# A chunked linear-attention kernel followed by a squared-relu feed-forward: eight heads at once, attention and feed-forward in one pipeline, x kept in SBUF

## The chip, the cores and the metric

The kernel runs on one core of a Trainium2 chip. The metric is device time in microseconds (us). Profiles are taken by the hardware profiler on the same core; a profile's span is about 2 us shorter than the device time.

Engines, as the profile names them: PE is TensorE's matmuls, PEld its weight loads, DVE is VectorE, ACT is ScalarE, POOL is GpSimd, SP is SyncE, which only issues DMA here. SBUF is the on-chip memory that tiles live in, PSUM the one that this program's matmuls write to, HBM the large memory that loads come from. A *slot* is one pass of the changed kernel's main loop.

## The reference

Four batches, eight heads, 768 tokens, head dimension 48. Attention keeps one 48x48 state per batch and head; its output is reshaped to x (3072 tokens by 384) and goes through two matrices.

```python
for t in range(S):                                       # attention, r k v: (4, 8, 768, 48)
    cur = einsum('bhd,bhe->bhde', u * k[t], v[t])        # the bonus term
    y[t] = einsum('bhd,bhde->bhe', r[t], state + cur)
    state = w * state + einsum('bhd,bhe->bhde', k[t], v[t])
x = y.transpose(0, 2, 1, 3).reshape(3072, 384)
h = x @ w_in                                             # 384 x 2048
g = maximum(h, 0) ** 2
out = g @ w_out                                          # 2048 x 384
```

Both kernels compute attention in chunks of 128 tokens: scores inside a chunk by matmul and mask, earlier chunks by the state, the decay folded into r and k beforehand. A *unit* below is 128 tokens of one batch. There are 24 units, of eight heads each.

## The kernel before

One head at a time: 192 bodies like this one, with 48 columns in most operations.

```python
for c in range(NCH):
    for b in range(B):
        for h in range(H):
            nc.sync.dma_start(out=rt, in_=r[b, h, t0 : t0 + C, :])      # kt, vt alike
            nc.vector.tensor_tensor(Rw, rt, wp_pos[h], ALU.mult)        # 128 x 48
            nc.vector.tensor_tensor(Kd, kt, wp_neg[h], ALU.mult)
            nc.vector.tensor_tensor(rku, rt, kt, ALU.mult)
            # ... bonus sum du, transposes of Rw and Kd, copy to SBUF ...
            nc.tensor.matmul(out=AT_p, lhsT=KdT, rhs=RwT, start=True, stop=True)
            nc.vector.tensor_tensor(AT, AT_p, smask, ALU.mult)          # 128 x 128
            # ... diagonal, two output matmuls, state update ...
            nc.sync.dma_start(out=xT[...], in_=yT)                      # x goes to HBM
actx.close()
nc.gpsimd.dma_start(out=w_in_sb, in_=moe_w_in...)                       # weights only now
nc.gpsimd.dma_start(out=w_out_sb, in_=moe_w_out...)
for t in range(NG):                                                     # 6 groups of 512 tokens
    nc.sync.dma_start(out=xt, in_=xT[...])
    for f in range(NF):                                                 # 16
        # three matmuls 128x128x512 into hps
        nc.scalar.activation(gr, hps, AF.Relu)
        nc.vector.tensor_tensor(g, gr, gr, ALU.mult)
        # four matmuls 128x128x384 into ops
```

Of the kernel before, what the change touches and what calls it, by code (L numbers as in the profile page):

```python
# [8 lines left out]
F32 = mybir.dt.float32  # L9
BF16 = mybir.dt.bfloat16  # L10
# [5 lines left out]
def kernel(  # L16
# [11 lines left out]
    nc = tc.nc  # L28
# [3 lines left out]
    dm = H * D  # L32
    dff = moe_w_in.shape[1]
    ntok = B * S

    xT = nc.dram_tensor("xT_scratch", (dm, ntok), BF16, kind="Internal").ap()

    const = ctx.enter_context(tc.tile_pool(name="const", bufs=1))
    ident = const.tile([128, 128], F32)
    make_identity(nc, ident)  # L40
    identb = const.tile([128, 128], BF16)
    nc.vector.tensor_copy(identb, ident)
# [4 lines left out]
    iota_f = const.tile([128, 1], F32)  # L47
    nc.vector.tensor_single_scalar(iota_f, iota_i, 0.0, ALU.add)
    neg_ip1 = const.tile([128, 1], F32)
    nc.vector.tensor_scalar(neg_ip1, iota_f, -1.0, -1.0, ALU.mult, ALU.add)  # L50
    rev_i = const.tile([128, 1], F32)
    nc.vector.tensor_scalar(rev_i, iota_f, -1.0, float(C - 1), ALU.mult, ALU.add)

    hpool = ctx.enter_context(tc.tile_pool(name="hpool", bufs=1))
    wp_pos = []
    wp_neg = []
    wp_rev = []
    u_bc = []
    w128 = []
    for h in range(H):  # L60
        lnw = hpool.tile([128, D], F32, name=f"lnw{h}")
        w_row = w[h : h + 1, :]
        w_bc = bass.AP(tensor=w_row.tensor, offset=w_row.offset,
                       ap=[[0, 128], w_row.ap[1]])
        nc.sync.dma_start(out=lnw, in_=w_bc)
        nc.scalar.activation(lnw, lnw, AF.Ln)
        t_pos = hpool.tile([128, D], F32, name=f"wppos{h}")
        nc.vector.tensor_single_scalar(t_pos, lnw, iota_f, ALU.mult)
        nc.scalar.activation(t_pos, t_pos, AF.Exp)
        wp_pos.append(t_pos)  # L70
        t_neg = hpool.tile([128, D], F32, name=f"wpneg{h}")
        nc.vector.tensor_single_scalar(t_neg, lnw, neg_ip1, ALU.mult)
        nc.scalar.activation(t_neg, t_neg, AF.Exp)
        wp_neg.append(t_neg)
        t_rev = hpool.tile([128, D], F32, name=f"wprev{h}")
        nc.vector.tensor_single_scalar(t_rev, lnw, rev_i, ALU.mult)
        nc.scalar.activation(t_rev, t_rev, AF.Exp)
        wp_rev.append(t_rev)
        tu = hpool.tile([128, D], F32, name=f"ubc{h}")
        u_row = u[h : h + 1, :]  # L80
        u_bcast = bass.AP(tensor=u_row.tensor, offset=u_row.offset,
                          ap=[[0, 128], u_row.ap[1]])
        nc.sync.dma_start(out=tu, in_=u_bcast)
        u_bc.append(tu)
        tw = hpool.tile([D, 1], F32, name=f"w128_{h}")
        w_col = w[h : h + 1, :].rearrange("a d -> d a")
        nc.sync.dma_start(out=tw, in_=w_col)
        nc.scalar.activation(tw, tw, AF.Ln)
        nc.scalar.activation(tw, tw, AF.Exp, scale=float(C))
        w128.append(tw)  # L90

    actx = ExitStack()
    spool = actx.enter_context(tc.tile_pool(name="state", bufs=1))
    spool2 = actx.enter_context(tc.tile_pool(name="state2", bufs=1))
    lpool = actx.enter_context(tc.tile_pool(name="attn", bufs=6))
    ppool = actx.enter_context(tc.tile_pool(name="attn_psum", bufs=2, space=bass.MemoryType.PSUM))

    stf_l = {}
    st_l = {}
    for b in range(B):  # L100
        for h in range(H):
            stf_l[(b,h)] = spool.tile([D, D], F32, name=f"stf_{b}_{h}")
            st_l[(b,h)] = spool2.tile([D, D], BF16, name=f"st_{b}_{h}")
    for c in range(NCH):
        t0 = c * C
        for b in range(B):
            for h in range(H):
                stf = stf_l[(b,h)]
                st = st_l[(b,h)]
                rt = lpool.tile([C, D], F32)  # L110
                kt = lpool.tile([C, D], F32)
                vt = lpool.tile([C, D], BF16)
                nc.sync.dma_start(out=rt, in_=r[b, h, t0 : t0 + C, :])
                nc.sync.dma_start(out=kt, in_=k[b, h, t0 : t0 + C, :])
                nc.gpsimd.dma_start(out=vt, in_=v[b, h, t0 : t0 + C, :])  # L115

                Rw = lpool.tile([C, D], BF16)
                nc.vector.tensor_tensor(Rw, rt, wp_pos[h], ALU.mult)  # L118
                Kd = lpool.tile([C, D], BF16)
                nc.vector.tensor_tensor(Kd, kt, wp_neg[h], ALU.mult)  # L120
                Kd2 = lpool.tile([C, D], BF16)
                nc.vector.tensor_tensor(Kd2, kt, wp_rev[h], ALU.mult)
                rku = lpool.tile([C, D], F32)
                nc.vector.tensor_tensor(rku, rt, kt, ALU.mult)  # L124
                nc.vector.tensor_tensor(rku, rku, u_bc[h], ALU.mult)  # L125
                du = lpool.tile([C, 1], F32)
                nc.scalar.activation(rku, rku, AF.Copy, accum_out=du)  # L127

                tp = ppool.tile([D, 2, C], BF16, name="tp")
                nc.tensor.transpose(tp[:, 0, :], Rw, identb)  # L130
                nc.tensor.transpose(tp[:, 1, :], Kd, identb)  # L131
                RwKdT = lpool.tile([D, 2, C], BF16, name="RwKdT")
                nc.scalar.copy(RwKdT, tp)  # L133
                RwT = RwKdT[:, 0, :]
                KdT = RwKdT[:, 1, :]

                AT_p = ppool.tile([C, C], F32)
                nc.tensor.matmul(out=AT_p, lhsT=KdT, rhs=RwT, start=True, stop=True)  # L138
                AT = lpool.tile([C, C], BF16)
                nc.vector.tensor_tensor(AT, AT_p, smask, ALU.mult)  # L140
                dgt = lpool.tile([C, C], F32)
                nc.vector.tensor_single_scalar(dgt, ident, du, ALU.mult)  # L142
                nc.vector.tensor_tensor(AT, AT, dgt, ALU.add)  # L143

                yp = ppool.tile([D, C + D], F32, name="yp")
                yT_p = yp[:, :C]
                nc.tensor.matmul(out=yT_p, lhsT=vt, rhs=AT, start=True,  # L147
                                 stop=(c == 0))
                if c > 0:
                    nc.tensor.matmul(out=yT_p, lhsT=st, rhs=RwT, start=False,  # L150
                                     stop=True)
                yT = lpool.tile([D, C], BF16)
                nc.scalar.copy(yT, yT_p)  # L153
                nc.sync.dma_start(
                    out=xT[h * D : (h + 1) * D, b * S + t0 : b * S + t0 + C],
                    in_=yT,
                )

                skv_p = yp[:, C:]
                nc.tensor.matmul(out=skv_p, lhsT=Kd2, rhs=vt, start=True, stop=True)  # L160
                if c < NCH - 1:
                    if c == 0:
                        nc.scalar.copy(stf, skv_p)
                    else:
                        nc.vector.tensor_single_scalar(stf, stf, w128[h], ALU.mult)
                        nc.vector.tensor_tensor(stf, stf, skv_p, ALU.add)
                    nc.scalar.copy(st, stf)

    actx.close()

    wpool = ctx.enter_context(tc.tile_pool(name="wpool", bufs=1))
    w_in_sb = wpool.tile([128, 3, dff], BF16)
    nc.gpsimd.dma_start(out=w_in_sb,
                      in_=moe_w_in.rearrange("(ko ki) f -> ki ko f", ki=128))
    w_out_sb = wpool.tile([128, 16, dm], BF16)
    nc.gpsimd.dma_start(out=w_out_sb,
                      in_=moe_w_out.rearrange("(ko ki) f -> ki ko f", ki=128))

    mpool = ctx.enter_context(tc.tile_pool(name="moe", bufs=3))
    mps = ctx.enter_context(tc.tile_pool(name="moe_psum", bufs=1, space=bass.MemoryType.PSUM))  # L180
    mps2 = ctx.enter_context(tc.tile_pool(name="moe_psum2", bufs=2, space=bass.MemoryType.PSUM))
    NK = dm // 128
    NF = dff // 128
    TG = 512
    NG = ntok // TG

    for t in range(NG):
        xt = mpool.tile([128, NK, TG], BF16)
        nc.sync.dma_start(
            out=xt,  # L190
            in_=xT[:, t * TG : (t + 1) * TG].rearrange("(ko ki) n -> ki ko n", ki=128),
        )
        ops = [mps.tile([128, dm], F32, name=f"op{q}") for q in range(4)]
        for f in range(NF):
            hps = mps2.tile([128, TG], F32, name="hps")
            for kk in range(NK):
# [53 lines left out]
```

## Time and profile before

| | before |
|---|---|
| device time, median of 3 runs | 579.48 us (577.61 to 579.75) |
| span of the profile | 574.9 us |
| set-up, to the first steady attention | 0 to about 40 us |
| attention, 192 bodies | about 40 to 414 us |
| waiting for weights, then six groups 22.4 us apart | 414 to 575 us |

The page of the kernel before: span, busy time by engine, then the busy share in 40 equal slices (tenths; 9 is 90% or more).

```profile
span 574.9 us, 8757 instructions
PE 382.9 (67%) x1792; PEld 172.3 (30%) x1792; DVE 359.3 (62%) x1916; ACT 304.6 (53%) x1150; POOL 105.0 (18%) x203
...
PE   0006666676666666666666667676618999999995
DVE  1118777887878787887877777676503544544442
DMA  2102333333333233332332333232484202111011
```

The windows view of the same run, one row for each of the parts (busy us and number of instructions per engine, clock, DMA share, GB/s).

```profile
core 0: us, PE busy (x) PEld busy (x) DVE busy (x) ACT busy (x) POOL busy (x), PEclk, DMA share, GB/s
0.00:40.00 40.00, 0.65 (x3) 0.34 (x3) 6.02 (x35) 33.50 (x66) 4.47 (x15) 1.00 0.13 19
40.00:414.00 374.00, 246.01 (x1115) 108.59 (x1114) 287.65 (x1783) 204.56 (x964) 98.57 (x186) 1.00 0.31 40
414.00:440.00 26.00, 9.77 (x36) 4.25 (x37) 3.46 (x7) 2.78 (x6) 1.96 (x2) 1.00 0.80 143
440.00:575.00 135.00, 126.45 (x641) 59.15 (x638) 62.18 (x92) 63.73 (x116) 0.00 (x0) 0.99 0.13 44
```

In the attention stage, 374 us, no engine is full: VectorE is busiest with 77% (287.65 of 374.00). In the last 135 us PE is.

Three groups of VectorE instructions (line, engine, operation, tiles, shape, count; busy us, mean ns of one; idle time before them and its releaser).

```profile
L124 DVE TENSOR_TENSOR rku<-rt,kt 128x48 f32<-128x48 f32 x192 | 38.2, 199 | 0.0
L140 DVE TENSOR_TENSOR AT<-AT_p,smask 128x128 bf16<-128x128 f32 x192 | 55.4, 288 | 53.1 <-PE AT_p L138 51.4
L207 DVE TENSOR_TENSOR g<-gr 128x512 bf16<-128x512 f32 x96 | 64.9, 692 | 89.0 <-ACT gr L206 78.9
```

An operation of 48 columns takes 199 ns and one of 128 takes 288 ns: most of the cost of a narrow operation does not depend on its width. That is the case for eight heads in one operation.

The chain of waits between the two stages (start in us, length, what).

```profile
415.74 1.75 DMA xT_scratch<-yT
...
419.25 17.35 DMA w_out_sb<-in_moe_w_out_dram
```

The weights hold the chain for 17 us there. PE in the dense stage, from the timeline (start, length, engine, line, operation):

```profile
501.76 0.32 PE L209 MATMUL op_8071<-w_out_sb,g 128*128 128x384 bf16 x1
501.92 0.32 PE L209 MATMUL op_8072<-w_out_sb,g 128*128 128x384 bf16 x1
502.08 0.33 PE L209 MATMUL op_8073<-w_out_sb,g 128*128 128x384 bf16 x1
```

Starts count here, not lengths: matmuls overlap, and 384 columns take 0.16 us each.

### The profile page before, as it was taken

To read this page: it belongs to the slowest core of one execution; us is meant where nothing else is said; L and a number is where in the kernel's file an instruction comes from. 1 tells how busy PE (TensorE), PEld (TensorE's weight loads), DVE (VectorE), ACT (ScalarE), POOL (GpSimd) and SP (SyncE) were. 2 spreads that over 40 slices of the span, in tenths; PEclk is the share of its full clock that TensorE was granted. 3 is DMA by queue.
4 is the path that set the end of the run, shared out by engine and by line. 5 is a ranking of instruction groups with operands and counts; after the bars stand their busy time and mean duration, and the time that the engine had idled before them with its cause. 6 is when DMAs were issued, how large, how long until landed. Compare 5 with 4: busy or idle time off the path is not lost. (4 is left out here: it accounts for less than half of the span.)

```text
span 574.9 us, 8757 instructions
## 1 busy us (share of the span) xinstructions
PE 382.9 (67%) x1792; PEld 172.3 (30%) x1792; DVE 359.3 (62%) x1916; ACT 304.6 (53%) x1150; POOL 105.0 (18%) x203
## 2 busy tenths in 40 slices
PE   0006666676666666666666667676618999999995
PEld 0002222232223232322322223332203444444442
DVE  1118777887878787887877777676503544544442
ACT  5996666555555555555555555434303545445453
POOL 3002222222222222222222222222010000000000
PEclk9999999999999999999999999999999999999998
DMA  2102333333333233332332333232484202111011
GB/s 24 28 0 33 41 42 40 41 41 37 39 40 40 37 42 38 39 41 38 37 41 37 43 38 38 36 38 36 103 153 67 70 14 83 28 56 55 1 56 55
DMA packets 106422, 25.38 MB, mean 44 GB/s; under 512 B 98560, under 2 KB 105984, under 8 KB 106368
## 3 DMA queue, kind: packets, MB, share of 16 engines
q1 hardware_dynamic: 76256, 19.31, 15.5%
q0 software_dynamic: 30112, 5.52, 11.7%
q14 instruction: 40, 0.33, 0.2%
q8 instruction: 14, 0.23, 0.2%
HBM read 23.20 MB, written 7.08 MB: 53 GB/s over the span
## 5 line engine op out<-in xcount | busy, mean ns | idle before, releaser
L115 POOL DMA_DIRECT2D vt<-in_v_dram x192 | 101.9, 532 | 300.5 <-PE yp L160 194.1
L207 DVE TENSOR_TENSOR g<-gr 128x512 bf16<-128x512 f32 x96 | 64.9, 692 | 89.0 <-ACT gr L206 78.9
L133 ACT COPY RwKdT<-tp 48x256 bf16<-48x256 bf16 x192 | 70.3, 366 | 90.2 <-PE tp L131 89.2
L206 ACT ACTIVATE gr<-hps 128x512 f32<-128x512 f32 x96 | 57.5, 600 | 86.4 <-PE hps L197 85.2
L131 PE MATMUL tp<-identb,Kd 128*48 128x128 bf16 x192 | 57.5, 300 | 54.6 <-DVE Kd L120 54.2
L130 PE MATMUL tp<-identb,Rw 128*48 128x128 bf16 x192 | 56.8, 296 | 52.4 <-DVE Rw L118 51.7
L140 DVE TENSOR_TENSOR AT<-AT_p,smask 128x128 bf16<-128x128 f32 x192 | 55.4, 288 | 53.1 <-PE AT_p L138 51.4
L197 PE MATMUL hps<-xt,w_in_sb 128*128 128x512 bf16 x288 | 76.6, 390 | 14.2 <-DMA w_in_sb<-in_moe_w_in_dram 13.0
L138 PE MATMUL AT_p<-RwKdT 48*128 48x128 bf16 x192 | 54.6, 284 | 40.5 <-ACT RwKdT L133 38.8
L153 ACT CAST yT<-yp 48x128 bf16<-48x128 f32 x192 | 49.7, 259 | 50.8 <-issue 13.8
L147 PE MATMUL yp<-AT,vt 128*48 128x128 bf16 x192 | 52.9, 276 | 4.6 <-DVE AT L143 2.9
L143 DVE TENSOR_TENSOR AT<-AT,dgt 128x128 bf16<-128x128 bf16 x192 | 55.0, 286 | 0.1
L142 DVE TENSOR_SCALAR dgt<-ident,du 128x128 f32<-128x128 f32 x192 | 53.0, 276 | 0.4 <-ACT rku L127 0.2
L127 ACT ACTIVATE rku<-rku 128x48 f32<-128x48 f32 x192 | 46.4, 242 | 3.5 <-DVE rku L125 2.5
L131 PEld LDWEIGHTS <-Kd 128*48 128x48 bf16 x192 | 22.6, 118 | 82.6 <-DVE Kd L120 80.5
L130 PEld LDWEIGHTS <-Rw 128*48 128x48 bf16 x192 | 21.9, 114 | 82.7 <-DVE Rw L118 61.5
L209 PEld LDWEIGHTS <-g 128*128 128x128 bf16 x384 | 34.5, 97 | 40.0 <-DVE g L207 18.1
L138 PEld LDWEIGHTS <-RwKdT 48*128 48x128 bf16 x192 | 19.3, 100 | 82.5 <-ACT RwKdT L133 75.4
L197 PEld LDWEIGHTS <-w_in_sb 128*128 128x128 bf16 x288 | 28.5, 99 | 50.6 <-issue 25.8
L124 DVE TENSOR_TENSOR rku<-rt,kt 128x48 f32<-128x48 f32 x192 | 38.2, 199 | 0.0
L127 ACT ACTIVATION_READ_ACCUMULATOR rku<-rku 128x1 f32 x192 | 36.4, 190 | 0.0
L147 PEld LDWEIGHTS <-vt 128*48 128x48 bf16 x192 | 23.9, 124 | 13.3 <-issue 6.6
(933 smaller groups left out, 564.4 us busy)
## 6 DMA issues: line engine op xcount, KB each, us to landing
rt<-in_r_dram SPq DMA_DIRECT2D x192, 24.0 KB, 1.8
kt<-in_k_dram SPq DMA_DIRECT2D x192, 24.0 KB, 1.9
out_dram<-osb SPq DMA_DIRECT2D x24, 192.0 KB, 1.9
vt<-in_v_dram POOLq DMA_DIRECT2D x192, 12.0 KB, 2.0
xT_scratch<-yT SPq DMA_DIRECT2D x192, 12.0 KB, 1.4
xt<-xT_scratch SPq DMA_DIRECT2D x6, 384.0 KB, 3.5
w_in_sb<-in_moe_w_in_dram POOLq DMA_DIRECT2D x1, 1536.0 KB, 10.4
w_out_sb<-in_moe_w_out_dram POOLq DMA_DIRECT2D x1, 1536.0 KB, 17.4
```

The source lines that it names most:

```text
L115: nc.gpsimd.dma_start(out=vt, in_=v[b, h, t0 : t0 + C, :])
L127: nc.scalar.activation(rku, rku, AF.Copy, accum_out=du)
L130: nc.tensor.transpose(tp[:, 0, :], Rw, identb)
L131: nc.tensor.transpose(tp[:, 1, :], Kd, identb)
L133: nc.scalar.copy(RwKdT, tp)
L138: nc.tensor.matmul(out=AT_p, lhsT=KdT, rhs=RwT, start=True, stop=True)
L140: nc.vector.tensor_tensor(AT, AT_p, smask, ALU.mult)
L143: nc.vector.tensor_tensor(AT, AT, dgt, ALU.add)
L147: nc.tensor.matmul(out=yT_p, lhsT=vt, rhs=AT, start=True, stop=(c == 0))
L197: nc.tensor.matmul(out=hps, lhsT=w_in_sb[:, kk, f * 128 : (f + 1) * 128], rhs=xt[:, kk, :], start=(kk == 0), stop=(kk == NK - 1),)
L206: nc.scalar.activation(gr, hps, AF.Relu)
L207: nc.vector.tensor_tensor(g, gr, gr, ALU.mult)
```

## The change

The intent: do each elementwise step for all eight heads at once, move products of r and k to GpSimd, keep x in SBUF, load weights at the start, and put attention of chunk c, the first matmul of chunk c-1 and the second of chunk c-2 into one loop, so that PE always has dense work while attention waits for other engines. The new kernel, cut to its core:

```diff
+    aps = ... tile_pool(name="attn_psum", bufs=4, PSUM)      # all 8 banks: 4 + 2 + 2
+    hps_pool = ... bufs=2 ; ops_pool = ... bufs=2
+    for n in range(4):
+        load(n)                       # r, k, v of one unit: three DMAs, rows of 48 values
+    nc.gpsimd.dma_start(out=w_in_sb, in_=moe_w_in...)         # at the start now
+    nc.gpsimd.dma_start(out=w_out_sb, in_=moe_w_out...)
+    def s0(n):                        # one unit ahead; every operand 128 x 384
+        nc.gpsimd.tensor_tensor(rp[:, :, :D], rt, wr, ALU.mult)
+        nc.gpsimd.tensor_tensor(kp[:, :, :D], kt, wk, ALU.mult)
+        nc.scalar.copy(vb, vt)
+        nc.gpsimd.tensor_tensor(rk, rt, kt, ALU.mult)
+        nc.gpsimd.tensor_tensor(rk, rk, ub, ALU.mult)
+        nc.vector.tensor_reduce(du, rk, axis=X, op=ALU.add)
+        nc.gpsimd.tensor_tensor(dv, vt, du[:, :, None].to_broadcast([C, H, D]), ALU.mult)
+    def s1(n):                        # 8 transposes, 4 k-v matmuls, state
+        ...
+        nc.scalar.copy(rkT, rk_p)                             # 128 x 1024 from PSUM
+        nc.vector.tensor_tensor(sm, kv_p, states[b], ALU.add)
+        nc.gpsimd.tensor_tensor(sm, sm, wc, ALU.mult)
+        nc.scalar.copy(sb, sm)
+    def s2(n): ...                    # 8 score matmuls, VectorE masks them, 2 x 512
+    def s3(n): ...                    # 12 output matmuls, VectorE adds dv -> yb
+    def s4(n): ...                    # 3 transposes, ScalarE copies into xts[c]
+    def m1(c, f): ...                 # 3 matmuls of 512; relu; square gr * gr
+    def m2(c, b, part): ...           # 4 matmuls of 384
+    for slot in range(NU + 2 * B):    # 24 units + 8
+        g, j = divmod(slot, B)
+        if slot + 1 < NU: s0(slot + 1)
+        if slot + 4 < NU: load(slot + 4)
+        for part in range(4):
+            if slot < NU: attn[part](slot)                    # s1, s2, s3, s4
+            if 0 <= g - 1 < NCH: m1(g - 1, j * 4 + part)
+            if 0 <= g - 2 < NCH: m2(g - 2, j, part)
```

A scheduler orders each engine's instructions by when it reckons that they are ready.

## The prediction

> **What bounds the kernel now.** The busy-by-slice table shows three parts of the 574.9 us span. Until about 40 us it sets up: the timeline shows 24 small loads and thirteen 1.28 us activation-table loads (ScalarE busy 42 of the first 50 us). Until about 414 us attention runs, one head of 128 tokens at a time: 192 units at about 1.9 us. There no engine is full (windows table, 200 to 300 us: PE 65%, DVE 81%, ACT 55%), and the 48-wide operations are mostly fixed cost: DVE takes 199 ns for 48 columns, 288 for 128, 692 for 512. Each unit is a latency chain; VectorE is nearest to full. Then the chain of waits shows about 20 us for the weights, whose load could start only after attention, and six feed-forward groups 22.4 us apart. PE is full there: matmuls start 162 ns (384 columns) and about 215 ns (512) apart, so 288 and 384 of them need 124 us.
>
> **What the change does.** Eight heads share each elementwise operation, so 192 units become 24. Per unit: VectorE does 3 operations of 384 (about 555 ns, from a line through 199, 288, 692) and 2 of 512 from PSUM (692); ScalarE five copies (four of 384 at 0.48 us, one of 1024 at about 1.0 us); GpSimd now does five or six two-input products of 384. The scratch tensor and its 12 KB stores vanish, setup uses one table load per function, weights load under the first units. Feed-forward work is unchanged, but interleaved.
>
> **Cost of one full slot** (one unit plus a quarter of each matmul of a group):
> - PE: 124/24 = 5.2 us feed-forward, plus 35 small matmuls at 80 to 110 ns (close pairs in the attention timeline) = 3.2 us: 8.4 us.
> - VectorE: 3 x 0.555 + 2 x 0.69 + 4 x 0.69 (squares) = 5.8 us.
> - ScalarE: 4 x 0.60 + 4 x 0.48 + 1.0 = 5.4 us.
> - GpSimd: no product of this kind is in the trace. The Trainium skill, "GPSIMD Engine Reference", section 3.1, gives 4497 ns for 2048 elements; scaled, an estimate of 0.9 to 0.95 us each, 5.6 us. "SBUF — State Buffer", section "Who interferes with whom", says that a VectorE operation with two SBUF inputs and a GpSimd operation that reads SBUF exclude each other. The squares (2.8 us per slot) are such: 8.4 us on that shared port. Nothing in the trace of before shows this.
>
> PE and shared port are equal at 8.4; in-order waits between the four attention steps (ScalarE's 1.0 us copy, VectorE's two maskings) exceed the 1.3 us of feed-forward work put between them, adding 0.5 to 1 us. I expect 9.2 us.
>
> **Total.** Start-up to the first transposes 12 us; 4 slots of attention alone, latency-bound, 6.5 us each: 26; 4 slots without the second matmul, 8.5 each: 34; 16 full slots at 9.2: 147; 4 of feed-forward alone at 5.3: 21; 4 of the second matmul at 2.7: 11; tail 3. Sum 254 us. Nearly all the gain is on the critical path: attention goes under the matmuls. Range 222 to 292; faster by over 2% 0.985, same 0.01, slower 0.005.
>
> **What would show it.** Right: full slots of 8.5 to 10 us, PE starting something over 85% of the time, GpSimd busy over 60% in the middle, squares or GpSimd products longer than alone (squares above 692 ns), no second weight wait, PE waits before masked-score and transposed matmuls. Wrong, faster: no port exclusion, small matmuls at 60 ns: slots of 7.5, about 225 us. Wrong, slower: GpSimd products above 1.2 us (strided heads, blocking), VectorE stuck in order behind the bonus-term reduction that waits for GpSimd: slots of 11, about 285 us.

## The result, and the profile after

The changed kernel takes 275.44 us (median of 4, 274.84 to 275.95) against 579.22 us in the same rounds: a ratio of 0.4758, 95% interval 0.4749 to 0.4768. The result is inside the predicted range, 21 us above the point.

The page after, the rows that answer to those of before and GpSimd's:

```profile
span 273.1 us, 4008 instructions
PE 183.9 (67%) x1480; PEld 100.6 (37%) x1480; DVE 144.0 (53%) x224; ACT 124.3 (46%) x219; POOL 149.1 (55%) x147
...
PE   0002021345959493975868686699999999999994
DVE  3100132435899556785656474567666766655500
POOL 4004999769997797577965785677555300000000
DMA  5999999835341254234532424100000000010021
```

PE is no fuller than before on average, 67%. In the first third it waits, in the last it is full. DMA is full for about the first 50 us, and GpSimd is busy from about 27 us on.

The windows after. The bounds are: first transposes at 24.7 us; the first four units (attention alone) done at 66.2; the next four (no second matmul yet) at 101.1; the full slots until 237; then feed-forward alone. A unit is done when ScalarE starts the copy of its transposed output, read from the timeline.

```profile
core 0: us, PE busy (x) PEld busy (x) DVE busy (x) ACT busy (x) POOL busy (x), PEclk, DMA share, GB/s
0.00:24.70 24.70, 0.00 (x0) 0.00 (x0) 2.79 (x12) 5.03 (x8) 4.27 (x13) 1.00 1.00 167
24.70:66.20 41.50, 12.30 (x127) 9.04 (x128) 13.84 (x25) 10.35 (x18) 36.94 (x40) 1.00 0.88 167
66.20:101.10 34.90, 28.00 (x224) 14.57 (x222) 27.89 (x36) 18.85 (x34) 30.80 (x28) 0.90 0.35 72
101.10:209.50 108.40, 83.83 (x719) 44.53 (x717) 69.16 (x106) 57.81 (x106) 73.33 (x66) 0.97 0.26 60
209.50:237.00 27.50, 27.29 (x237) 14.73 (x236) 17.99 (x29) 17.29 (x29) 3.79 (x4) 1.00 0.08 30
237.00:273.00 36.00, 32.46 (x184) 17.71 (x181) 12.29 (x18) 14.93 (x27) 0.00 (x0) 0.99 0.14 50
```

Against the terms of the prediction:

| stretch | predicted us | measured us |
|---|---|---|
| start to the first transposes | 12 | 24.7 |
| four slots of attention alone | 26 | 41.5 |
| four slots without the second matmul | 34 | 34.9 |
| sixteen full slots | 147 | 135.9 |
| first and second matmul without attention | 21 | 22.1 |
| second matmul alone | 11 | 10.4 |
| tail | 3 | 3.6 |
| sum | 254 | 273.1 |

The sixteen full slots fall in three: eight of 9.6 us on average (101.1 to 177.8), four of 7.9 (to 209.5), four of 6.9 (to 237.0). In the last four GpSimd has nearly nothing left to do (3.79 us), and PE is busy all the time: 6.8 us, the length of the last three, is what PE's work alone takes.

The granted clock (PEclk) dips to 0.90 in one row and 0.97 in another. As a rival explanation it is worth little: the four runs of this kernel had mean clocks of 0.974 once and 0.95 three times, and their times differ by at most 1.1 us.

Two findings stand in the groups of the page. The squares are longer than the 692 ns of before, and GpSimd's products differ in length, also within one group: `rk` from 984 to 1447 ns.

```profile
L246 DVE TENSOR_TENSOR g<-gr 128x512 bf16<-128x512 f32 x96 | 80.4, 846 | 53.9 <-ACT gr L245 53.9
...
L149 POOL TENSOR_TENSOR dv<-vt,du 128x384 f32<-128x384 f32 x24 | 25.5, 1064 | 39.2 <-DVE yb L219 31.4
...
L144 POOL TENSOR_TENSOR rk<-rt,kt 128x384 f32<-128x384 f32 x24 | 27.7, 1157 | 2.0 <-DVE du L147 2.0
```

The third shows in the timeline of one slot of 10 us, here with VectorE's, ScalarE's and GpSimd's instructions that hand on to each other (start, length, engine, line, operation, tiles; in brackets the engine's idle time before it and what ended it).

```profile
156.93 0.55 DVE L219 TENSOR_TENSOR yb<-y_p,dv 128x384 bf16<-128x384 f32 x1
157.56 1.21 POOL L149 TENSOR_TENSOR dv<-vt,du 128x384 f32<-128x384 f32 x1 [2.31 <-DVE yb L219]
158.80 0.55 DVE L147 TENSOR_REDUCE du<-rk 128x8 f32<-128x384 f32 x1 [0.72 <-POOL dv L149]
159.43 1.38 POOL L144 TENSOR_TENSOR rk<-rt,kt 128x384 f32<-128x384 f32 x1 [0.67 <-DVE du L147]
160.89 1.00 POOL L145 TENSOR_TENSOR rk<-rk,ub 128x384 f32<-128x384 f32 x1
161.33 1.10 DVE L246 TENSOR_TENSOR g<-gr 128x512 bf16<-128x512 f32 x1 [0.91 <-ACT gr L245]
161.85 1.44 POOL L139 TENSOR_TENSOR rpad_142<-rt,wr 128x384 bf16<-128x384 f32 x1
163.26 0.99 POOL L140 TENSOR_TENSOR kpad_143<-kt,wk 128x384 bf16<-128x384 f32 x1
164.21 0.99 POOL L179 TENSOR_TENSOR sm_1585<-sm_1585,wc 128x384 f32<-128x384 f32 x1
165.24 0.51 ACT L181 CAST sb_1588<-sm_1585 128x384 bf16<-128x384 f32 x1 [3.94 <-POOL sm_1585 L179]
165.66 0.59 ACT L245 ACTIVATE gr<-hps 128x512 f32<-128x512 f32 x1
166.28 0.69 DVE L246 TENSOR_TENSOR g<-gr 128x512 bf16<-128x512 f32 x1 [2.64 <-ACT gr L245]
166.89 0.55 DVE L219 TENSOR_TENSOR yb<-y_p,dv 128x384 bf16<-128x384 f32 x1
```

Follow it down. The output add `yb` of one unit frees a `dv` buffer, so GpSimd may start the `dv` of a later unit. That frees a `du` buffer for the reduction, which frees an `rk` buffer for the next product. Then GpSimd works through its list, and the state product `sm` of the unit at hand stands last in it. ScalarE has been waiting 3.94 us for this with the state cast, and the relu behind the cast in its order has waited along, the square behind the relu, and the next `yb` behind the square. From `yb` to `yb` it is 9.96 us. GpSimd is busy 7.01 of these (1.21 + 1.38 + 1.00 + 1.44 + 0.99 + 0.99). This is a ring of waits, with no engine full. It was followed in this one slot. The three slots of 9.95 us from 148 to 178 us end in the same wait, and the longest one (12.6 us, from 101 us) has it too (4.50 us for `sm`); the four slots of 8.1 to 8.8 us between them were not followed.

### The profile page after: what moved, and what is told of

It is laid out like the page before. It is cut to its first block, busy times and chain, and to the rows that moved or that the text cites. A ratio compares the mean times of both kernels' runs of the same rounds, so it can differ in the third digit from the quotient of the medians.

```text
span 273.1 us, 4008 instructions
## 1 busy us (share of the span) xinstructions
PE 183.9 (67%) x1480; PEld 100.6 (37%) x1480; DVE 144.0 (53%) x224; ACT 124.3 (46%) x219; POOL 149.1 (55%) x147
## 3 DMA queue, kind: packets, MB, share of 16 engines
q1 hardware_dynamic: 78480, 19.08, 32.6%
## 5 line engine op out<-in xcount | busy, mean ns | idle before, releaser
L246 DVE TENSOR_TENSOR g<-gr 128x512 bf16<-128x512 f32 x96 | 80.4, 846 | 53.9 <-ACT gr L245 53.9
L239 PE MATMUL hps<-xt,w_in_sb 128*128 128x512 bf16 x288 | 85.2, 402 | 12.7 <-ACT gr L245 12.7
L255 PE MATMUL ops<-w_out_sb,g 128*128 128x384 bf16 x384 | 76.9, 329 | 0.0
L149 POOL TENSOR_TENSOR dv<-vt,du 128x384 f32<-128x384 f32 x24 | 25.5, 1064 | 39.2 <-DVE yb L219 31.4
L147 DVE TENSOR_REDUCE du<-rk 128x8 f32<-128x384 f32 x24 | 13.2, 550 | 44.4 <-POOL rk L145 35.2
L214 PE MATMUL y_p<-vb,AT 128*128 128x48 bf16 x192 | 16.9, 196 | 18.2 <-DVE AT L198 17.8
L144 POOL TENSOR_TENSOR rk<-rt,kt 128x384 f32<-128x384 f32 x24 | 27.7, 1157 | 2.0 <-DVE du L147 2.0
L142 ACT CAST vb<-vt 128x384 bf16<-128x384 f32 x24 | 12.2, 508 | 34.5 <-DMA vt<-in_v_dram 17.3
L170 ACT COPY rkT<-rk_p 128x1024 bf16<-128x1024 bf16 x24 | 24.3, 1013 | 3.9 <-PE rk_p L163 1.4
L145 POOL TENSOR_TENSOR rk<-rk,ub 128x384 f32<-128x384 f32 x24 | 24.5, 1024 | 1.0
L160 PE MATMUL rk_p<-identb,rpad_134 128*128 128x128 bf16 x32 | 3.6, 242 | 24.7 <-POOL rpad_134 L139 24.7
L232 ACT COPY xt<-yt_p 128x384 bf16<-128x384 bf16 x24 | 11.5, 479 | 15.1 <-PE yt_p L231 14.9
L261 ACT COPY osb<-ops 128x384 f32<-128x384 f32 x24 | 11.5, 478 | 9.4 <-PE ops L255 8.5
L219 DVE TENSOR_TENSOR yb<-y_p,dv 128x384 bf16<-128x384 f32 x24 | 13.3, 552 | 3.9 <-PE y_p L214 3.8
## 6 DMA issues: line engine op xcount, KB each, us to landing
w_in_sb<-in_moe_w_in_dram POOLq DMA_DIRECT2D x1, 1536.0 KB, 14.8
```

Source lines behind the costliest of these rows:

```text
L144: nc.gpsimd.tensor_tensor(rk, rt, kt, ALU.mult)
L145: nc.gpsimd.tensor_tensor(rk, rk, ub, ALU.mult)
L147: nc.vector.tensor_reduce(du, rk, axis=mybir.AxisListType.X, op=ALU.add)
L149: nc.gpsimd.tensor_tensor(dv, vt, du[:, :, None].to_broadcast([C, H, D]), ALU.mult)
L170: nc.scalar.copy(rkT, rk_p)
L214: nc.tensor.matmul(out=y_p[:, p, i, :], lhsT=q["AT"][:, i, p, :], rhs=q["vb"][:, 2 * p + i, :], start=(c == 0), stop=True, skip_group_chec ...
```

## The experiments

All gave correct outputs. Each was timed in three rounds. The times are medians, the ratios are to the kernel before in the same rounds; 0.4758 is the changed kernel's.

| run | us | ratio to before, 95% interval |
|---|---|---|
| changed kernel | 275.44 | 0.4758 (0.4749 to 0.4768) |
| e1_late_weights | 264.99 | 0.4575 (0.4555 to 0.4595) |
| e2_cast_late | 275.15 | 0.4753 (0.4732 to 0.4775) |
| e3_six_buffers | 272.03 | 0.4698 (0.4684 to 0.4713) |
| e4_square_from_psum | 255.95 | 0.4423 (0.4408 to 0.4437) |
| e5_state_on_vector | 263.95 | 0.4554 (0.4538 to 0.4569) |
| e6_three_together | 231.41 | 0.3999 (0.3984 to 0.4014) |
| e7_serial | 320.81 | 0.5542 (0.5523 to 0.5561) |
| e8_before_weights_early | 570.67 | 0.9853 (0.9825 to 0.9881) |
| e9_weights_held | 221.95 | 0.3833 (0.3821 to 0.3846) |
| e10_bonus_in_order | 223.82 | 0.3874 (0.3848 to 0.3899) |
| e11_bonus_two_buffers | 220.80 | 0.3818 (0.3805 to 0.3832) |
| e12_held_alone | 253.40 | 0.4381 (0.4364 to 0.4397) |

### The start: e1_late_weights and e12_held_alone

```diff
-    nc.gpsimd.dma_start(out=w_in_sb, ...)      # before the pads are made
-    nc.gpsimd.dma_start(out=w_out_sb, ...)
     for slot in range(NU + 2 * B):
+        if slot == 1: nc.gpsimd.dma_start(out=w_in_sb, ...)
+        if slot == 2: nc.gpsimd.dma_start(out=w_out_sb, ...)
```

> The two weight loads are issued with the second and third attention unit instead of before the first. In the changed kernel the load of the first unit's v lands at 22.5 us, behind 3 MB of weights, and the decay tables wait behind its cast, so the first transposes start at 24.7 us. Theory (weights crowd out the first loads): first v lands by about 13 us, first matmul at 14 to 17 us, total 275 down to 263 to 268 us. Rival (the start is hidden, because GpSimd or the slots after it set the pace anyway): first matmul earlier, but the total within 2 us of 275.

The first v landed at 8.8 us, not 22.5, and the first transposes came at 12.3 us, not 24.7. The total fell by 10.4 us. So the crowding is real and reaches the end. But the first weight load still went out at 9.1 us, since a program place does not hold a DMA back that is ready, and the third unit's loads waited behind it. e12 holds the loads by a dependency instead: a one-column copy into the weight tile, which the load then overwrites. The copy reads the padded keys of the second unit, and for the second matrix those of the fifth (the text of e9 says the sixth). The loads went out at 17.5 and 32.7 us.

```diff
+        if slot == 1:
+            nc.gpsimd.tensor_copy(w_in_sb[:, 0, 0:1], kpads[1][:, 0, 0:1])
+            nc.gpsimd.dma_start(out=w_in_sb, ...)
+        if slot == 4:
+            nc.gpsimd.tensor_copy(w_out_sb[:, 0, 0:1], kpads[1][:, 0, 0:1])
+            nc.gpsimd.dma_start(out=w_out_sb, ...)
```

> The changed kernel with nothing but the weight loads held back as above; square and state product as they were. Loads theory: the start gains as in the three-together pair (some 10 us against late weights by program order, which gave 265.0 us): 254 to 258 us. If the ring on GpSimd and VectorE sets the pace after the start whatever the loads do, 262 to 266 us.

It gave 253.40 us, 22 us less than the changed kernel with no compute operation changed but for the two one-column copies. That is slightly better than the 254 to 258 us expected. In the windows of e12, the stretch from the first transposes to the fourth unit's end:

```profile
12.50:44.80 32.30, 12.25 (x127) 8.99 (x128) 12.38 (x22) 9.58 (x16) 31.46 (x36) 1.00 1.13 196
```

The same work took 41.50 us in the changed kernel. The start gained 12.2 us and the four slots 9.2 us. All these loads share the DMA engines whatever queue they come from, as the Trainium skill says ("Trainium Kernel Development and Optimization", section Key Constraints); the trace agrees: the first unit's k, issued from another queue than the weights, landed at 17.1 us with them in flight and at 8.0 us without.

### A cast that did not move: e2_cast_late

```diff
     def s0(n):
-        nc.scalar.copy(vb, vt)
     def s1(n):
+        nc.scalar.copy(vb, vt)
```

> The cast of v moves from the preparation of a unit (one unit ahead) to the unit's own first step; loads stay as they are. Theory (ScalarE's order costs it: the decay tables and the first score copy sit behind casts that wait for loads that land at 22.5, 28.7 and 31.6 us): the decay tables are made at about 14 us, the first score matmul comes at about 25 us instead of 33.1, total 266 to 271 us. Rival (the crowded loads alone set the start): first score matmul within 2 us of 33, total within 2 us of 275.

Nothing changed: 275.15 us, first score matmul at 33.09 us. But the run does not tell what it was made for. Its trace shows ScalarE's order as before, the cast of the first v still ahead of the decay tables (22.51 and 22.93 us): the scheduler puts it there wherever the program has it. Whether that order costs anything beside the late landing stays untested; e12 shows that with early loads the question is moot.

### The shared port: e4_square_from_psum and e7_serial

```diff
-        nc.vector.tensor_tensor(gs[c][:, f]..., gr, gr, ALU.mult)
+        nc.vector.tensor_tensor(gs[c][:, f]..., gr, hps, ALU.mult)
```

> The square is taken as relu(h) from SBUF times h from PSUM, so that no VectorE operation in the slots has two SBUF inputs; same count and size. Theory (exclusion on the port that VectorE and GpSimd share): squares all at 680 to 700 ns (now 30 of 96 are longer, mean 846), GpSimd products all at 0.8 to 1.0 us (now up to 1.45), the ring of 10.0 us loses about 1.2 us, total 266 to 271 us. Rival (the longer squares and products have another cause): the durations stay spread and the total within 2 us of 275; h is held longer in its two PSUM buffers, which may cost 1 to 3 us.

relu(h) times h is relu(h) squared, so the result is the same; one operand now comes from PSUM. The groups of e4:

```profile
L246 DVE TENSOR_TENSOR g<-gr,hps 128x512 bf16<-128x512 f32 x96 | 65.8, 686 | 55.9 <-ACT gr L245 55.6
...
L144 POOL TENSOR_TENSOR rk<-rt,kt 128x384 f32<-128x384 f32 x24 | 23.9, 996 | 2.7 <-DVE du L147 2.7
```

Every square takes 676 to 690 ns, where the longest took 1508 ns, and no GpSimd product exceeds 1006 ns, where the longest took 1455 ns. The total fell by 19.5 us, more than the 4 to 9 us expected, and the cost feared (h held longer) shows as 8.0 us of PE waiting for squares, which did not outweigh the gain. In sum, the changed kernel's 96 squares were 14.8 us longer than 692 ns each, and its 136 products 18.2 us longer than in e4.

A second, independent check is e7, in which feed-forward never runs beside attention. There GpSimd's products are short with the old square:

```profile
L144 POOL TENSOR_TENSOR rk<-rt,kt 128x384 f32<-128x384 f32 x24 | 23.8, 992 | 0.0
```

This is the rule that the Trainium skill gives in "SBUF — State Buffer", section "Who interferes with whom": a VectorE instruction with two SBUF inputs and a GpSimd instruction that reads SBUF exclude each other, and which one waits depends on who came first. The trace agrees on both sides. e6 below agrees too: there the 16 state products are the only VectorE operations left with two SBUF inputs. They take up to 1410 ns (557 at least), and 14 of GpSimd's 120 products again exceed 1010 ns.

### The ring: e3_six_buffers and e5_state_on_vector

```diff
-    apool = ctx.enter_context(tc.tile_pool(name="attn", bufs=3))
+    apool = ctx.enter_context(tc.tile_pool(name="attn", bufs=6))
```

> Attention's temporary tiles get 6 buffers instead of 3; the work is the same. Theory (the 10.0 us slots are a ring of waits: output add, bonus product, its reduction, next products, state product, state cast, relu, square, output add, closed by the three buffers): the ring opens, the slots of chunks 2 to 4 fall from 8.7 to 10.0 us to about 8, total 263 to 269 us. Rival (GpSimd and the port that it shares with VectorE are simply full there): slots unchanged, total within 2 us of 275.

It fell by 3.4 us, between the two expectations. The slots that took 10.0 us took 8.6. GpSimd's wait for `yb` before `dv` went from 31.4 to 16.4 us in total, so the buffers had closed part of the ring. But ScalarE still waited 40.8 us for state products (45.8 us in the changed kernel). More buffers let GpSimd run further ahead; they do not move the one urgent product forward in its list. e5 takes that product out of the list:

```diff
-                nc.gpsimd.tensor_tensor(sm, sm, wc, ALU.mult)
+                nc.vector.tensor_tensor(sm, sm, wc, ALU.mult)
```

> The decay product of the state moves from GpSimd to VectorE, all else as in the changed kernel. Theory (in-order ring: ScalarE's state cast, and the relus behind it, wait 3.9 us a slot for a GpSimd product that stands behind four products for later units): that wait goes, the 10.0 us slots fall to 8 to 8.5 us, total 262 to 268 us. Rival (the shared port is full and sets the slot; the product's place does not matter, and on VectorE it has two SBUF inputs and excludes GpSimd too): slots above 9 us, total above 271 us.

It gave 263.95 us, 11.5 us less, though the moved product now has two SBUF inputs on VectorE and the exclusion remains (37 squares above 750 ns). ScalarE's idle time before state casts fell from 48.9 to 18.4 us. The slots that took 10.0 us took 8.5 to 9.1. So the ring, and not a full port or a full GpSimd, set these slots. But e5 takes the product off GpSimd altogether: it does not tell the product's place at the end of the list from the list being one product (0.99 us in the slot shown) shorter. No run kept the product on GpSimd and moved it forward, so that the place alone matters is argued, not shown.

### Together, and how far it goes: e6, e9, e10, e11

e6 has the edits of e1, e4 and e5.

> Late weights, square with one PSUM input and state product on VectorE together. If the three causes are separate, the gains add: late weights 10.4 and square 19.5 us as measured, state product 6 to 12 us: 234 to 240 us, full slots near the 6.8 us that the last four full slots show. If the state product only moves the same wait, 244 to 247 us.

It gave 231.41 us, 44 us less, better than the 234 to 240 us expected; the three gains alone sum to 41.4. After the thirteenth unit slots are 6.8 to 7.3 us, and from 123 to 193 us PE is busy 69.0 of 69.5 us: this part is bound by PE. What remains is at the start. e9 adds the held loads of e12 to it:

> As the three together (231.4 us), but each weight load is really held back: a one-column copy from the padded keys of the second unit (and of the sixth) into the weight tile goes first, so the load of the first matrix can be issued only at about 17 us, of the second at about 35 us. In the three together the first weight load still went out at 9.1 us and unit 3's k landed at 21.2 us, the fourth attention unit ended at 54.5 us. Theory (the loads of the first units decide the first four slots): fourth unit done by 40 to 46 us, total 217 to 225 us. Rival (VectorE waiting in order for GpSimd products made for later units decides them): fourth unit still past 50 us, total 228 to 232 us; a weight that now comes too late would show as matmuls waiting for its landing.

It gave 221.95 us. The fourth unit ended at 45.1 us (54.5 in e6), and from then on it is the same kernel. e10 and e11 also move the bonus term (two products, reduction, `dv`) from s0, one unit ahead, into the unit's own s2, with one or two buffers for `rk`:

```diff
     def s2(n):
         q = unit[n]
+        bonus(n)                   # rk, rk*u, du, dv: formerly in s0
...
-        rk = apool.tile([C, H, D], F32, name="rk")
+        rk = apool.tile([C, H, D], F32, name="rk", bufs=1)     # e11: bufs=2
```

> As the weights held back, and the bonus term (two products, reduction, product) is written into the unit's own second step, with one buffer for its product, so that GpSimd and VectorE have less of later units' work ahead of the present one. Theory of the rival above (in-order waits for run-ahead work): another 3 to 10 us less than the weights held back alone. If loads alone decide: within 2 us of it, or slower by 1 to 3 us because one buffer makes GpSimd wait for the reduction.

> As the last one, with two buffers for the bonus product instead of one. With one buffer the fourth unit ended at 40.3 us against 45.1 us, but units 10 to 13 then took 10.6, 6.4 and 11.0 us. If the single buffer caused these, two buffers keep the early gain and lose the late stall: 215 to 220 us. If the stall is that of the second weight matrix or of the order itself, 222 to 226 us as with one.

In e10 the fourth unit ended at 40.3 us, 27.6 us after the first transposes: run-ahead work on GpSimd, for which VectorE waits in order, had cost 5 us there. But units eleven to thirteen (10.6, 6.4 and 11.0 us) lost it again; there VectorE waited for the `rk` of the reduction (6.8 us) and PE for VectorE to free h (6.6 us). So its total fits the second expectation (loads alone decide), though the early gain does not. With two buffers those three slots took 5.2 to 7.1 us, yet the fifth unit took 11.8 us, and the total lies between the two expectations. The intervals of e9 and e11 overlap (0.3821 to 0.3846, 0.3805 to 0.3832): the two are not told apart. e10 is slower than e11. What sets the first units in e11 is not settled. 220 to 222 us, about 0.80 of the changed kernel's time (0.3818 / 0.4758), is the best found.

### What the parts of the change are worth: e7_serial and e8_before_weights_early

e7 keeps everything of the change but the interleaving. Feed-forward takes its PSUM from the banks that attention gives back, which makes it serial. (Whether writing the loops one after the other would have been enough is not shown.)

```diff
+    actx = ExitStack()             # aps is opened in it
     for slot in range(NU):
         ...  for part in range(4): attn[part](slot)
+    actx.close()                   # h_psum and o_psum are opened only here
+    for slot in range(NU + B):
+        ...  m1(g, j * 4 + part); m2(g - 1, j, part)
```

> The changed kernel without interleaving: all 24 attention units first, the feed-forward after (its PSUM tiles take the banks that attention gives back), x still in SBUF. It tells what interleaving is worth. Theory: 25 us start, 24 units at 6.5 to 7.9 us (one latency chain each, as in the first four slots), then 124 us of dense matmuls plus 6: 320 to 345 us, so interleaving is worth 45 to 70 us and the batching of heads some 240. Rival (batching alone gives nearly all): below 300 us.

It gave 320.81 us. So eight heads at a time, x in SBUF and the early weights bring 579 to 321 us together (no run tells these apart), and interleaving brings the last 45 us. In e7 attention alone runs at 6.1 us a unit once it is under way. That is near GpSimd's time (five products of 0.99 us, one of 0.83), and GpSimd is busy 94% from 72 to 145 us. But from 150 to 188 us it is busy 29% and the units still take 5.9 to 6.1 us, so GpSimd alone does not set this pace; what does is open. Interleaving could have hidden up to 131 us of feed-forward; it hid 45. The later edits brought another 53 (275.44 to 221.95 in e9), of which part is the shorter start and not better hiding.

e8 is the kernel before with its two weight loads moved ahead of attention.

> The kernel before, with nothing changed but that the two weight loads are issued before attention. Its trace shows some 20 us between the last attention unit and the first steady feed-forward group, spent on the weights. Theory: 555 to 562 us. Rival (the scratch round trip or the first loads take it back, as crowded loads did in the changed kernel's start): above 570 us.

It gave 570.67 us: 8.2 us less, not 17 to 25. The 17 us wait between the stages is gone from its chain of waits, but attention now ends at 421.3 us instead of 415.7 (end of the last copy `yT`): the small set-up loads land behind the weights, the last of them at 32.6 us instead of 19.0. That is 5.6 of the some 9 us missing; the rest was not followed. Moving a load does not remove it. This is the same effect as in e1, from the other side.

## Why the prediction was right or wrong

- "Start-up to the first transposes 12 us": wrong by 12.7 us. The failed step is "weights load under the first units", as if for free. They crowd out the first units' loads. With loads held back the start was 12.5 us (e12), so the rest of the estimate was right. (A slip beside it: the trace of before has 22 activation-table loads in the first 43 us, not thirteen.)
- "4 slots of attention alone, latency-bound, 6.5 us each": 10.4 us each. They were not bound by their latency but by loads (9.2 of the 15.5 us, e12), and by GpSimd and VectorE working in order on later units' bonus terms (about 5 us, e9 against e10). With both out of the way it is 6.9 us a slot (e10).
- "the squares ... exclude each other" with GpSimd's products: right, with the right mechanism and 30 of 96 squares clearly longer than alone (over 700 ns). The estimate of 8.4 us on that port could not be tested as a bound, since the slots were bound otherwise. Its effect on the total was 19.5 us (e4).
- "an estimate of 0.9 to 0.95 us each" for GpSimd's products: 0.99 us alone, 0.83 us for `dv`, whose second operand is broadcast. The estimate from the Trainium skill ("GPSIMD Engine Reference", section 3.1) was 4 to 9% short.
- "35 small matmuls at 80 to 110 ns = 3.2 us": wrong. A slot that only PE binds takes 6.8 us, and 5.2 of these are feed-forward; 31 small matmuls took the other 1.6 us, 52 ns each. The spacing was read from the attention stage of before, for which that trace holds no clock record (its first is at 435.0 us). In the timeline after, next to dense matmuls, they start 50 ns apart:

```profile
169.20 0.22 PE L163 MATMUL rk_p<-identb,kpad_135 128*128 128x128 bf16 x1
169.25 0.21 PE L165 MATMUL kv_p<-vb,kpad_135 128*128 128x96 bf16 x1
169.30 0.22 PE L163 MATMUL rk_p<-identb,kpad_135 128*128 128x128 bf16 x1
```

  In the same kernel at 26 us, with attention alone, the same pair starts 90 to 100 ns apart. The Trainium skill ("TensorE: Matmul & The Clock Gate", Part 1) has 107 ns for 128 columns with a cold array and 56 ns with a warm one. The spacings fit that, and the trace shows the cause. Its clock row reads 1.00 in both places, but its first clock record is at 71.2 us; before that there is nothing to read. Where a record says half, the wide spacing is back in the middle of a full slot:

```profile
139.50:142.90 3.40, 3.40 (x21) 1.62 (x20) 1.69 (x3) 2.19 (x4) 3.40 (x4) 0.50 0.49 123
...
139.71 0.31 PE L163 MATMUL rk_p<-identb,kpad_135 128*128 128x128 bf16 x1
139.81 0.29 PE L165 MATMUL kv_p<-vb,kpad_135 128*128 128x96 bf16 x1
139.90 0.31 PE L163 MATMUL rk_p<-identb,kpad_135 128*128 128x128 bf16 x1
```

  The first row is the windows view, with a granted clock of 0.50; the other lines are the timeline. In this stretch matmuls of 512 columns start 427 ns apart, against 215 outside it. They also start some 425 ns apart from 67 to 71 us, before the first record. So the prediction's 80 to 110 ns belong to half the clock. For the stretch at 26 us and for the attention stage of before this is inferred from the spacing, since no record covers them.
- "I expect 9.2 us" a full slot: 8.5 us on average, but as a mixture. Eight slots took 9.6 us, the longest of them because of the ring, which the prediction named only as a risk ("VectorE stuck in order behind the bonus-term reduction"), four took 7.9 and four 6.9 us. PE's 8.4 us were about 1.5 too many, and for in-order waits only 0.5 to 1 us stood in the sum. This error, 11 us too much in all, hid part of the 28 us missed at the start; that the total came within 21 us of the point is in part luck.
- "PE starting something over 85% of the time": missed: PE was busy 77% in the window from 101 to 209 us, 82% over all sixteen full slots. "GpSimd busy over 60% in the middle": right, 73% from 66 to 209 us.
- "Nearly all the gain is on the critical path: attention goes under the matmuls": only partly. Most of the gain is that attention itself became cheaper. Per 128 tokens of eight heads it took 15.6 us before (374 us over 24) and takes 6.1 us in e7; hiding it brought 45 us.

## What to carry to other kernels

Moving work to an idle engine pays less if its results are needed by engines that wait in order: look where in that engine's list the urgent result stands, and whether buffers and in-order waits close a ring in which no engine is full. A two-input VectorE operation that can take one input from PSUM leaves GpSimd alone. And a bulk load that is needed late must be held back by a real dependency, since here neither a later place in the program nor another queue kept the weights from taking the DMA engines from the loads that were needed first.

## What the Trainium skill lacked or had wrong

- "TensorE: Matmul & The Clock Gate", section "Back-to-back issue gap": it gives a sustained 81 ns for a pair of weight load and matmul at 128 columns, and 131 ns at 512. Here such pairs of 96 to 128 columns start 50 ns apart between dense matmuls (31 of 48 to 128 columns take 52 ns each on average), and those of 512 columns about 215 ns apart. The formula for an isolated matmul on the same page (N/2.4 + 2.5 ns: 56 and 216) fits better.
- "GPSIMD Engine Reference", section 3.1: of the two-input product it measures one length, 2048. A product of 384 columns takes 0.99 us here, 0.83 us if one operand is a value broadcast over 48 columns; no page has the second.
- "SBUF — State Buffer", section "Who interferes with whom": its exclusion is confirmed (squares of 692 ns reach 1508 ns, products of 996 ns reach 1455 ns), and so is its statement that a VectorE instruction with at most one SBUF input does not contend, which is the remedy of e4 (squares 676 to 690 ns). Nothing was lacking here; the prediction cited the rule and did not use the remedy.
- That all queues share the DMA engines is stated (see e12), but no page that I found gives what bulk weight loads cost the small loads issued before or beside them: the first unit's k landed at 17.1 us with them and at 8.0 us without.
